# RWKV-6 attention and an MLP on one core: the first level of the decay tree of rounds 3 to 7 moves from the natural layout on GpSimd and VectorE back to TensorE

## The chip, the cores and the metric

The kernel runs on one core of a Trainium2 chip. The metric is device time in microseconds (us) of one launch, from inputs in the chip's memory to the output there; lower is better.

## The reference

Two blocks, one after the other, all in float32. The first is a linear attention with a state that decays per channel; its output, with the heads side by side, is the input of a layer norm, a ReLU MLP and a residual sum.

```python
# r, k, v, w: (4, 8, 768, 48); u: (8, 48); state: (4, 8, 48, 48), zero at first
for t in range(S):
    kt, vt, rt, wt = (k[:, :, t], v[:, :, t], r[:, :, t], w[:, :, t])
    cur = einsum('bhd,bhe->bhde', u[None] * kt, vt)
    y[:, :, t] = einsum('bhd,bhde->bhe', rt, state + cur)
    state = wt[:, :, :, None] * state + einsum('bhd,bhe->bhde', kt, vt)
x = y.transpose(0, 2, 1, 3).reshape(4, 768, 384)
mu, var = mean and variance of x over its last axis
xn = (x - mu) / sqrt(var + 1e-6) * g_ln
out = x + maximum(xn @ w_ch1, 0) @ w_ch2        # w_ch1: 384 x 1536, w_ch2: 1536 x 384
```

## The kernel before

**Units, rounds, levels.** A unit is four heads of one batch over half a sequence (384 steps); a round is the two units that make up all eight heads of those 384 steps, so there are 8 rounds (0 to 7) of units 2·round and 2·round + 1. Inside a unit the sequence is cut into chunks of 64 steps. What step s of a chunk gets from an earlier step t of the same chunk is the product r(s)·k(t), damped by the decays between them, and the kernel builds these 64 x 64 matrices (`A`) in six levels, like a tree. At level `lev` with n = 2^lev, neighbouring blocks of n steps are joined: `quads` (line 477) multiplies the keys with the queries of every second block on TensorE, 24 products for a unit (two matmul instructions each) into the PSUM tile `a_ps`; `grow` (497) multiplies the block's decays into `rkT` in place on VectorE; `keep` (514) takes from `a_ps` the entries that belong to this level and puts them into `A`. `totals` (391) multiplies the decays of pairs of blocks, level by level, on GpSimd.

**Around the levels.** `states` (578) forms the products k·v of each chunk (PSUM tile `kv`) and carries the state from chunk to chunk on VectorE (tile `s`); `outputs` (634) multiplies `A` with v and r with the states (PSUM tile `y`). Two PSUM buffers (pool `ps_a`) are taken in turn by `a_ps`, `kv` and `y`. The term with u of the same step is made in the natural layout, with the steps on the partitions: `own_products` (409) makes r·u·k on GpSimd, `own_sums` (423) reduces it on VectorE, `own_term` (460) multiplies the sums with v on GpSimd. From unit 2 on the inputs are loaded twice: natural (`load`, 122) and as runs that VectorE transposes (`stage`, 150; `squares`, 359).

**Level 0 in the natural layout.** From round 3 on (`FIRST = 3`, line 798), level 0 is not done by `quads`. Level 0 joins a step with the step before it, with no decay in between, and so it is an own term with k and v of the step before. `load_before` (170) loads k, and later v, shifted by one step, into the two buffers `nat["w"]`; `own_products` multiplies the shifted k with r; `own_sums` reduces it into `next` and zeroes the even steps with `odd`; `own_term` multiplies `next` with the shifted v and adds the result to `vo`. `keep` of level 0 then only zeroes the odd columns of `A`, once for each of its two buffers (rounds 3 and 4).

**The order.** Nearly everything is issued through wrappers that keep program order on its engine (`InOrder`, 39); only the loads and stores on SyncE's queue are ordered by the scheduler of the framework. The order is written out by hand: for each round (line 899) and each level (903), together a slot, numbered (round - 1)·6 + level, come the states or outputs of the round before, the quads of this level, `grow`, `keep`, and then a list of tasks for later rounds, which `fill` (766) spreads between steps of the MLP of the round before. An MLP step is six matmuls or so; a slot of the later rounds holds four. The MLP's first half is written to PSUM tile `h_ps`, the second to `o_ps`.

The places that the change touches in this order are the condition ahead of `quads` (916), the two loads of level 3 (977 to 979) and the two of the last level (994, 996).

Of the kernel before, what the change touches and what calls it, by code (L numbers as in the profile page):

```python
# [9 lines left out]
F32 = mybir.dt.float32  # L10
# [5 lines left out]
ALU = mybir.AluOpType  # L16
AX = mybir.AxisListType
# [35 lines left out]
def kernel(  # L53
# [13 lines left out]
    PE, ACT, DVE, POOL, SPO = (  # L67
        InOrder(tc, e) for e in (nc.tensor, nc.scalar, nc.vector, nc.gpsimd, nc.sync)
    )
    SP = nc.sync  # L70

    B, H, S, D = r.shape
    P = 128
    HP = 64
    C = 64
    NH = 4
    NP = NH // 2
    U = H // NH
    TT = 3
    RN = TT * P  # L80
# [13 lines left out]
    const = ctx.enter_context(tc.tile_pool(name="const", bufs=1))  # L94
    p1 = ctx.enter_context(tc.tile_pool(name="p1", bufs=1))
    p2 = ctx.enter_context(tc.tile_pool(name="p2", bufs=2))
# [10 lines left out]
    units = [(b, f, g) for b, f in rounds for g in range(U)]  # L107
# [3 lines left out]
    nat = {  # L111
        nm: [const.tile([P, TT, NH, HP], F32, name=f"nat_{nm}{i}") for i in range(2)]
        for nm in "wkr"
    }
# [35 lines left out]
    def stage(q, nm, pr, eng=SP):  # L150
# [4 lines left out]
        for j in range(2):  # L155
            first = src.offset + ((b * H + g * NH + 2 * pr + j) * S + f * RN) * D
            for e in range(HP // SQ):
# [8 lines left out]
                        tensor=src.tensor, offset=first + SQ * e, ap=[[NS * D, SQ], [1, n]]  # L166
                    ),
                )

    def load_before(q, src, i, eng=SP):  # L170

        b, f, g = units[q]
        for c in range(TT):
            eng.dma_start(
                out=nat["w"][i][:, c, :, 0:D],
                in_=bass.AP(
                    tensor=src.tensor,
                    offset=src.offset + ((b * H + g * NH) * S + f * RN + c * P - 1) * D,
                    ap=[[D, P], [S * D, NH], [1, D]],
                ),  # L180
            )

    def load_v(q, eng=SP):
        vn[q] = p4.tile([P, TT, NH, D], F32, tag="v", name=f"v{q}")
# [21 lines left out]
    for j in range(2):  # L206
        ACT.dma_start(
            out=sel[ds(HP * j, D), :, j], in_=u.rearrange("(r j) d -> j d r", j=2)[j]
# [4 lines left out]
    ident = const.tile([P, P], F32, name="ident")  # L213
# [11 lines left out]

    a_bufs = [const.tile([P, 2, U, NK, C], F32, name=f"A{i}") for i in range(2)]
    for t in a_bufs:
# [4 lines left out]
    for lev in range(NLEV - 1):  # L232
# [3 lines left out]
        for base, sign in ((0, 1), (n - 1, -1)):  # L236
            POOL.affine_select(
                out=m, in_=m, compare_op=ALU.is_ge, fill=0.0, base=base,
# [10 lines left out]
        out=bits0, in0=masks[0].rearrange("p q n -> p (q n)"), scalar1=-1.0, scalar2=None,  # L249
        op0=ALU.mult,  # L250
# [94 lines left out]
    st, carry = {}, {}  # L345
# [63 lines left out]
    def own_products(q, eng):  # L409
        b, f, g = units[q]  # L410
        rk = st[q]["ruk"] = p1.tile([P, TT, NH, D], F32, tag="rk", name=f"rk{q}")
        eng.tensor_tensor(
            out=rk, in0=nat["k"][q % 2][..., 0:D], in1=nat["r"][q % 2][..., 0:D], op=ALU.mult
        )
        eng.tensor_tensor(
            out=rk, in0=rk,
            in1=u_bc[:, ts(g, NH)][:, None].broadcast_to([P, TT, NH, D]), op=ALU.mult,
        )
        if q >= FIRST * U:
            k1 = nat["w"][0][..., 0:D]  # L420
            eng.tensor_tensor(out=k1, in0=k1, in1=nat["r"][q % 2][..., 0:D], op=ALU.mult)

    def own_sums(q):
        o = st[q]["own"] = p4.tile([P, TT, NH], F32, tag="own", name=f"own{q}")
        DVE.tensor_reduce(out=o, in_=st[q]["ruk"], axis=AX.X, op=ALU.add)
        if q >= FIRST * U:

            o = st[q]["next"] = p2.tile([P, TT, NH], F32, tag="next", name=f"next{q}")
            DVE.tensor_reduce(out=o, in_=nat["w"][0][..., 0:D], axis=AX.X, op=ALU.add)
            DVE.tensor_scalar(out=o, in0=o, scalar1=odd, scalar2=None, op0=ALU.mult)  # L430

    def products(q, eng=DVE):
        a = st[q]
# [26 lines left out]
    def own_term(q, eng):  # L460
        a = st[q]
        a["vo"] = p4.tile([P, TT, NH, D], F32, tag="vo", name=f"vo{q}")
        eng.tensor_tensor(
            out=a["vo"], in0=vn[q],
            in1=a["own"][:, :, :, None].broadcast_to([P, TT, NH, D]), op=ALU.mult,
        )
        if q >= FIRST * U:
            v1 = nat["w"][1][..., 0:D]
            eng.tensor_tensor(
                out=v1, in0=v1,  # L470
                in1=a["next"][:, :, :, None].broadcast_to([P, TT, NH, D]), op=ALU.mult,
            )
            eng.tensor_tensor(out=a["vo"], in0=a["vo"], in1=v1, op=ALU.add)

    a_ps = {}

# [36 lines left out]

    def keep(rnd, lev):
        n = 1 << lev
        A = a_bufs[rnd % 2]
        if lev == 0 and rnd >= FIRST:

            if rnd < FIRST + 2:
                DVE.memset(  # L520
                    A.rearrange("s j u k (q two) -> s (j u k) q two", two=2)[..., 1], 0.0
                )
            return
        ps = a_ps[rnd]
        if lev == NLEV - 1:
            for j in range(2):
                for i in range(2):
                    rows = ds(C * i, n)
                    late.append((A[rows, j, :, :, n:], ps[rows, j]))
        elif lev == 0:  # L530

            DVE.tensor_tensor(
                out=A.bitcast(I32).rearrange("s j u k (q two) -> s j (u k) q two", two=2)[..., 1],
                in0=ps.bitcast(I32).rearrange("s j u k q -> s j (u k) q"),
                in1=bits0[:, None, None].broadcast_to([P, 2, U * NK, C // 2]),
                op=ALU.bitwise_and,
            )
        else:
            DVE.copy_predicated(
                out=A.rearrange("s j u k (q two n) -> s j (u k) q two n", two=2, n=n)[:, :, :, :, 1],  # L540
                mask=masks[lev][:, None, None].broadcast_to([P, 2, U * NK, C // (2 * n), n]),
                data=ps.rearrange("s j u k (q n) -> s j (u k) q n", n=n),
            )
        if lev == NLEV - 1:
            for q in units_of(rnd):

                a = st[q]
                a["rx"] = p2.tile([P, NK, C], F32, tag="rx", name=f"rx{q}")
                R = a["r"].rearrange("p (k i t) -> p k i t", i=2, t=C)
                for j in range(2):  # L550
                    late.append((a["rx"][ds(HP * (1 - j), HP)], R[ds(HP * j, HP), :, 1, :]))
# [232 lines left out]
    def each(f, *ranges):  # L784
        calls = [()]
        for r_ in ranges:
            calls = [c + (x,) for c in calls for x in r_]
        return [lambda c=c: f(*c) for c in calls]
# [5 lines left out]
    def units_of(rnd):  # L794
        return [U * rnd + g for g in range(U)] if rnd < NR else []


    FIRST = 3
    odd = const.tile([P, 1], F32, name="odd")

    def take(eng, q):

        own_products(q, eng)
# [95 lines left out]
    for rnd in range(1, NR + 1):  # L899
        old, now, new = units_of(rnd - 1), units_of(rnd), units_of(rnd + 1)  # L900
        if rnd == 1:
            old = []
        for lev in range(NLEV):
            slot = (rnd - 1) * NLEV + lev
# [8 lines left out]
                if lev >= U and now:  # L913
                    mlp_step()
            for q in now:
                if slot and (lev or rnd < FIRST):
                    quads(q, lev)
            for which in ("rk",) if lev < NLEV - 1 else "kr":
                for q in now:
# [5 lines left out]
            tasks = []  # L925
            if rnd == 1:
                if lev < 2:
                    tasks += each(load, new, "kr"[lev], [SPO])
                if lev == 2:
                    SPO.dma_start(  # L930
                        out=u_bc,
                        in_=bass.AP(
                            tensor=u.tensor, offset=u.offset, ap=[[0, P], [D, H], [1, D]]
# [6 lines left out]
                    own_term(now[lev - 4], POOL)  # L940
            if rnd == 2 and lev == 0:
                tasks += each(load_v, now)
                DVE.tensor_reduce(
                    out=odd, in_=ident.rearrange("p (q two) -> p q two", two=2)[:, :, 1],
                    axis=AX.X, op=ALU.add,
                )
            if rnd == 2 and lev == 2:
                for q in now:
                    take(DVE, q)
# [22 lines left out]
            if lev == 3 and rnd > 1:  # L972
                for q in now:
                    load_vx(q)
                for q in new:
                    load_v(q)
                if new:
                    load_before(new[0], k, 0)
                    load_before(new[0], v, 1)
                if rnd > 2:  # L980
                    moments(rnd - 1)
                    tasks = each(norm, [rnd - 1]) + tasks
# [4 lines left out]
            if lev == NLEV - 1:  # L987

                if now:
                    mlp_step()  # L990
                if rnd >= 2 and new:
                    own_sums(new[0])
                if rnd >= 2:
                    tasks += each(load_before, new[1:], [k], [0])
                    tasks += each(own_term, new[:1], [POOL])
                    tasks += each(load_before, new[1:], [v], [1])
                    tasks += each(own_products, new[1:], [POOL])
                    tasks += each(own_sums, new[1:]) + each(own_term, new[1:], [POOL])
                    if new:
                        tasks += each(totals, [rnd + 1], [POOL])  # L1000
                if now:
                    tasks = mixed(
                        tasks,
                        each(ends, now, pairs) + each(finish, [2, 2, 4])
                    )
                if rnd == 1:
                    tasks = [join] * JOINS[lev] + tasks + each(totals, [rnd + 1], [POOL])
# [43 lines left out]
```

## Time and profile before

| | |
|---|---|
| median of 5 runs | 565.99 us (564.19 to 566.18) |
| profiled execution | 566.0 us, its span 564.3 us |
| TensorE busy (PE) | 546.9 us, 97% |
| VectorE busy (DVE) | 332.7 us, 59% |
| ScalarE busy (ACT) | 168.8 us, 30% |
| GpSimd busy (POOL) | 135.6 us, 24% |
| mean granted TensorE clock | 0.991 of full speed |

The span runs from the first to the last instruction of one profiled execution; the profiled execution's own time is 1.7 us longer. Every instruction is issued by one helper line (49), so groups of instructions are told apart by tile names and shapes: `a_ps<-rkT` are the quads, `rkT<-rkT,wT` and `rkT<-rkT,tot` are `grow`, `nat_w` is the buffer of the shifted k and v. A group's row gives busy us, mean ns of one, and after the second bar the idle time of the engine ahead of these instructions with what ended it. PE is TensorE's matmuls, PEld its weight loads, SPq SyncE's queue of DMA issues. The chain of waits is followed back from the last instruction; its rows are start us, length us, engine and tile.

### The profile page before, as it was taken

Reading aid. Unit: us, or ns where it says so; the run is one execution under the profiler, and the core shown is the slowest. Engines: PE = TensorE matmul, PEld = TensorE weight load, DVE = VectorE, ACT = ScalarE, POOL = GpSimd, SP = SyncE. Lnnn points to the kernel's source line nnn. Section 1 sums busy time; section 2 is a strip of 40 time slices with the busy share of each in tenths; the row PEclk is TensorE's granted clock in tenths of the full one; section 3 lists DMA queues with packets and bytes.
Section 4 is the critical chain, followed back from the end, with each engine's and each line's share of the span. In section 5 each row is a group of like instructions: output and inputs, shape, how many; then the busy total and the mean of one; then the engine's idle time right before and its main releaser. Section 6 shows DMA issues by size and latency. Waiting matters only on the chain.

```text
span 564.3 us, 18202 instructions
## 1 busy us (share of the span) xinstructions
PE 546.9 (97%) x7898; PEld 358.6 (64%) x7898; DVE 332.7 (59%) x654; ACT 168.8 (30%) x363; POOL 135.6 (24%) x157
## 2 busy tenths in 40 slices
PE   8999998998889999999999999999999999999997
PEld 6776665675556666666666666666666666665554
DVE  4888998859777785757387655666572611130000
ACT  2576887502250015201421026201521025202200
POOL 6140010204194019401580029022640000000000
PEclk9899999999997999999999999999999999999999
DMA  9958887245566565646464646546200000000000
GB/s 230 183 141 163 190 217 187 61 89 105 126 154 141 126 127 121 135 110 140 96 138 100 139 107 137 118 112 124 58 1 2 31 15 1 2 29 15 0 15 28
DMA packets 141552, 56.64 MB, mean 100 GB/s; under 512 B 124448, under 2 KB 130720, under 8 KB 141472
## 3 DMA queue, kind: packets, MB, share of 16 engines
q1 hardware_dynamic: 139600, 54.88, 43.6%
q8 instruction: 62, 1.02, 0.8%
q10 hardware_dynamic: 1872, 0.59, 0.4%
q14 instruction: 18, 0.15, 0.1%
HBM read 48.66 MB, written 4.72 MB: 95 GB/s over the span
## 4 chain that ended last, share of the span: by engine, by line
PE 82%; DVE 8%; ACT 3%; DMA 2%; SPq 2%; issue 2%; POOL 0%; ACTq 0%; DVEq 0%; POOLq 0%
PE o_ps L49 33%; PE h_ps L49 27%; PE a_ps L49 9%; PE y L49 4%; DVE rkT L49 2%; DVE w_sb L49 2%; PE kv L49 2%; PE kn_ps L49 2%; SPq L163 1%; ACT rest L49 1%; DMA nat_r<-in_r_dram 1%; PE xT_ps L49 1%; PE own_ps L49 1%; PE k_ps L49 1%; PE r_ps L49 1%
## 5 line engine op out<-in xcount | busy, mean ns | idle before, releaser
L49 PE MATMUL o_ps<-w_sb,h 128*128 128x384 f32 x576 | 199.7, 496 | 1.0 <-ACT h L49 1.0
L49 PE MATMUL h_ps<-xT,w_sb 128*128 128x384 f32 x576 | 196.5, 491 | 2.8 <-DVE o L49 1.4
L49 PEld LDWEIGHTS h_ps<-xT,w_sb 128*128 128x128 f32 x576 | 105.8, 190 | 70.4 <-DVE o L49 2.0
L49 PEld LDWEIGHTS o_ps<-w_sb,h 128*128 128x128 f32 x576 | 106.6, 192 | 67.3 <-ACT h L49 2.3
L49 DVE TENSOR_TENSOR rkT<-rkT,tot 128x768 f32<-128x768 f32 (+1 forms) x96 | 77.8, 852 | 27.7 <-issue 17.6
L49 ACT ACTIVATE h<-h_ps 128x384 f32<-128x384 f32 x96 | 46.9, 488 | 142.6 <-PE h_ps L49 142.4
L49 PEld LDWEIGHTS a_ps<-rkT 48*64 48x64 f32 x4128 | 65.6, 136 | 23.6 <-issue 12.1
L49 PE MATMUL a_ps<-rkT 48*64 48x32 f32 x4128 | 70.6, 222 | 3.5 <-DVE rkT L49 3.4
L49 DVE TENSOR_TENSOR o<-o_ps,x 128x384 f32<-128x384 f32 x24 | 13.3, 555 | 96.4 <-PE o_ps L49 96.3
L49 POOL TENSOR_TENSOR vo<-v,own 128x576 f32<-128x576 f32 x16 | 19.3, 1207 | 102.0 <-DVE own L49 60.7
L49 ACT ACTIVATE rstd<-mv,eps 128x3 f32<-128x3 f32 x8 | 2.4, 296 | 133.4 <-DVE mv L49 133.4
L49 POOL TENSOR_TENSOR nat_w<-nat_w,nat_r 128x576 f32<-128x576 f32 x10 | 15.8, 1578 | 105.2 <-DMA nat_w<-in_v_dram 71.4
L49 DVE SCALAR_TENSOR_TENSOR s<-s,decay,kv 128x48 f32<-128x48 f32 x160 | 29.3, 258 | 18.9 <-PE kv L49 18.9
L49 DVE COPY_PREDICATED A<-mask,a_ps 128x768 f32<-128x768 int8 x32 | 38.4, 1199 | 0.0
L49 DVE TENSOR_TENSOR x<-y,vo 128x288 f32<-128x288 f32 x32 | 13.2, 453 | 34.3 <-PE y L49 34.3
L49 ACT ACTIVATE xT<-xT_ps,g_sb 128x384 f32<-128x384 f32 x24 | 13.6, 579 | 48.4 <-PE xT_ps L49 48.4
L49 DVE TENSOR_TENSOR rkT<-rkT,wT 128x768 f32<-128x768 f32 x16 | 24.9, 1592 | 0.9 <-PE a_ps L49 0.8
L49 DVE TENSOR_REDUCE own<-rk 128x12 f32<-128x576 f32 x12 | 9.0, 750 | 23.5 <-POOL rk L49 23.5
L49 DVE TENSOR_SCALAR w_sb<-w_sb 128x384 f32<-128x384 f32 (+1 forms) x48 | 19.6, 408 | 0.8
L49 PEld LDWEIGHTS y<-v,A 64*64 64x64 f32 x384 | 12.8, 135 | 7.6 <-issue 4.4
L49 POOL TENSOR_TENSOR tot<-wT 128x768 f32<-128x768 f32 x6 | 12.4, 2074 | 21.1 <-DVE rkT L49 21.1
L49 PEld LDWEIGHTS kv<-v,kn 64*64 64x64 f32 x768 | 12.7, 135 | 7.5 <-issue 6.4
(88 smaller groups left out, 546.0 us busy)
## 6 DMA issues: line engine op xcount, KB each, us to landing
raw<-in_moe_w_ch_dram SPq DMA_DIRECT2D x24, 384.0 KB, 3.6
w_runs<-in_w_dram SPq DMA_DIRECT2D x79, 70.0 KB, 2.1
k_runs<-in_k_dram SPq DMA_DIRECT2D x79, 70.0 KB, 2.0
r_runs<-in_r_dram SPq DMA_DIRECT2D x79, 70.0 KB, 2.0
v<-in_v_dram SPq DMA_DIRECT2D x48, 96.0 KB, 3.0
out_dram<-o SPq DMA_DIRECT2D x24, 192.0 KB, 2.5
nat_r<-in_r_dram SPq DMA_DIRECT2D x42, 96.0 KB, 3.3
nat_k<-in_k_dram SPq DMA_DIRECT2D x42, 96.0 KB, 3.3
```

What stands on the lines that cost most here:

```text
L49: return lambda *args, **kw: self.tc.keep_in_program_order(f(*args, **kw))
L163: eng.dma_start(out=t[ds(HP * j + SQ * e, SQ), 0:n], in_=bass.AP(tensor=src.tensor, offset=first + SQ * e, ap=[[NS * D, SQ], [1, n]]),)
```

## The change

`FIRST` and all that hangs on it are removed. `quads` of level 0 and `keep` of level 0 (`A` from `a_ps` and a bit mask) run in rounds 3 to 7 as they do in rounds 0 to 2. The shifted loads, the second product, the second sum, the scaling by `odd`, and the two further operations of the own term go, with the constant `odd` and its one reduction, and with the two memsets of `A`. The rest of the order stays as written.

```diff
-    def load_before(q, src, i, eng=SP):
-        b, f, g = units[q]
-        for c in range(TT):
-            eng.dma_start(out=nat["w"][i][:, c, :, 0:D], in_=bass.AP(...))
...
     def own_products(q, eng):
...
-        if q >= FIRST * U:
-            k1 = nat["w"][0][..., 0:D]
-            eng.tensor_tensor(out=k1, in0=k1, in1=nat["r"][q % 2][..., 0:D], op=ALU.mult)
     def own_sums(q):
...
-        if q >= FIRST * U:
-            o = st[q]["next"] = p2.tile([P, TT, NH], F32, tag="next", name=f"next{q}")
-            DVE.tensor_reduce(out=o, in_=nat["w"][0][..., 0:D], axis=AX.X, op=ALU.add)
-            DVE.tensor_scalar(out=o, in0=o, scalar1=odd, scalar2=None, op0=ALU.mult)
     def own_term(q, eng):
...
-        if q >= FIRST * U:
-            v1 = nat["w"][1][..., 0:D]
-            eng.tensor_tensor(
-                out=v1, in0=v1,
-                in1=a["next"][:, :, :, None].broadcast_to([P, TT, NH, D]), op=ALU.mult,
-            )
-            eng.tensor_tensor(out=a["vo"], in0=a["vo"], in1=v1, op=ALU.add)
     def keep(rnd, lev):
         n = 1 << lev
-        A = a_bufs[rnd % 2]
-        if lev == 0 and rnd >= FIRST:
-            if rnd < FIRST + 2:
-                DVE.memset(
-                    A.rearrange("s j u k (q two) -> s (j u k) q two", two=2)[..., 1], 0.0
-                )
-            return
-        ps = a_ps[rnd]
+        A, ps = a_bufs[rnd % 2], a_ps[rnd]
...
-    FIRST = 3
-    odd = const.tile([P, 1], F32, name="odd")
...
             for q in now:
-                if slot and (lev or rnd < FIRST):
+                if slot:
                     quads(q, lev)
...
             if rnd == 2 and lev == 0:
                 tasks += each(load_v, now)
-                DVE.tensor_reduce(
-                    out=odd, in_=ident.rearrange("p (q two) -> p q two", two=2)[:, :, 1],
-                    axis=AX.X, op=ALU.add,
-                )
...
                 for q in new:
                     load_v(q)
-                if new:
-                    load_before(new[0], k, 0)
-                    load_before(new[0], v, 1)
...
                 if rnd >= 2:
-                    tasks += each(load_before, new[1:], [k], [0])
                     tasks += each(own_term, new[:1], [POOL])
-                    tasks += each(load_before, new[1:], [v], [1])
                     tasks += each(own_products, new[1:], [POOL])
```

## Prediction

> **What bounds the kernel now.** I read the page's busy shares first, then its slices, then the groups by line and shape, and last the chain of waits and the windows around the only stretch where the slices dip in mid-run.
>
> ```profile
> PE 546.9 (97%) x7898; PEld 358.6 (64%) x7898; DVE 332.7 (59%) x654; ACT 168.8 (30%) x363; POOL 135.6 (24%) x157
> PE   8999998998889999999999999999999999999997
> PEclk9899999999997999999999999999999999999999
> ```
>
> PE is the bound: 547 of 564 us. The slices (14.1 us each) say where the other 17 us are: slices 9 to 11 (127 to 169 us) show 8, from slice 12 on all is 9. The second line is the granted clock; slice 12 (169 to 183 us) has 7.
>
> ```profile
> L49 PE MATMUL a_ps<-rkT 48*64 48x32 f32 x4128 | 70.6, 222 | 3.5 <-DVE rkT L49 3.4
> L49 POOL TENSOR_TENSOR nat_w<-nat_w,nat_r 128x576 f32<-128x576 f32 x10 | 15.8, 1578 | 105.2 <-DMA nat_w<-in_v_dram 71.4
> L49 POOL TENSOR_TENSOR vo<-vo,nat_w 128x576 f32<-128x576 f32 x10 | 14.1, 1406 | 0.8
> L49 DVE TENSOR_REDUCE next<-nat_w 128x12 f32<-128x576 f32 x10 | 7.5, 748 | 3.9 <-POOL nat_w L49 2.6 <-DMA w_runs<-in_w_dram 1.3
> L49 DVE TENSOR_TENSOR A<-a_ps,bits 128x768 int32<-128x768 int32 x3 | 2.9, 952 | 0.0
> ```
>
> These rows price the exchange (busy us in total, then mean ns of one). `a_ps` is what `quads` writes: 4128 matmuls are 86 calls of 48 (16 units by 6 levels, less the ten that rounds 3 to 7 skip), so 70.6/86 = 0.82 us a call. The `nat_w` and `next` rows go; the `bits` row, `keep` at level 0, comes five times more.
>
> The chain of waits over the whole span shows what a call costs in its place:
>
> ```profile
> 218.25 0.84 PE kv L49 x48
> 219.10 7.94 PE h_ps L49 x24
> 227.04 0.84 PE kv L49 x48
> 227.88 1.39 PE a_ps L49 x96
> 229.27 7.94 PE h_ps L49 x24
> 240.88 1.53 PE a_ps L49 x96
> ```
>
> This is round 4 (slots 18 and 19). PE never waits here; the chain is PE after PE. In slot 18 `states` (kv) goes straight to the MLP; in slot 19 the quads of level 1 stand between. They take 1.39 us for both units, and the MLP's 24 matmuls after them the same 7.94. After an MLP matmul the same 96 take 1.53.
>
> The chain asked for 140 to 184 us shows the dip:
>
> ```profile
> 157.65 0.84 DVE rkT L49
> ...
> 159.43 3.04 DMA nat_w<-in_k_dram
> ...
> 162.59 1.42 POOL nat_w L49
> ...
> 164.03 0.76 DVE next L49
> ...
> 165.13 1.99 DVE s L49 x12
> 167.12 3.70 DVE rkT L49 x2
> ...
> 170.86 1.51 PE a_ps L49 x48
> 172.37 8.07 PE o_ps L49 x18
> ```
>
> The load of the shifted k for unit 7 is issued last in SP's queue, behind 32 run loads; POOL multiplies it, DVE's in-order queue stands at `next`, and `s` (the states of round 2) and `grow` of round 3 stand behind it. The PE timeline there has two idle gaps before `a_ps`, 1.84 us (to 168.81) and 1.15 (to 170.86), both put down to DVE rkT. Windows over the same place, the eighth figure being the clock:
>
> ```profile
> 168.50:172.00 3.50, 2.04 (x92) 1.96 (x94) 3.39 (x7) 0.00 (x0) 3.34 (x3) 0.67 0.61 132
> 172.00:174.00 2.00, 2.00 (x19) 1.33 (x15) 2.00 (x10) 0.69 (x2) 0.91 (x4) 0.50 0.65 122
> ```
>
> The clock falls to half after these gaps. It is back to 1.00 in the window from 178 us.
>
> **The change part by part.** *Added on PE.* Level 0 returns in rounds 3 to 7: ten `quads`, 480 matmuls, right behind `states(old[0])` in slots 12, 18, 24, 30 and 36. From 172 to 459 us PE has no idle, so every added us counts. I take 1.39 a round, as the nearest row (slot 19) is the same sequence kv, a_ps, h_ps: 5 x 1.39 = 6.95. Bounds: 1.39, and 1.53 plus the 0.19 that six o_ps take more after a_ps than otherwise (2.13 against 1.94), 1.72 a round or 8.6 in all.
>
> *Removed from PE's waits in slot 12.* Both gaps, 1.84 + 1.15 = 2.99 us, hang on `next`, which goes with its load. Rebuilt: DVE ends the last `squares` of unit 7 at 160.93 (it starts at 160.06, 0.87 long, held by the r runs, which SP issues ahead of the removed load, so it stays). `own_sums(7)` follows with no wait, as POOL needs 1.15 for vo from 155.1 and 1.42 + 1.40 for the products: 159.1. Then 0.75, `s` 2.0, so 163.7; two `grow` of level 0 at the slow 1.9 us each beside POOL's totals (3.77 the pair at 285 us), 167.5; `keep` 0.95, 168.5.
>
> PE meanwhile: kv ends 159.78, quads of unit 6 take 0.70, and those of unit 7 wait for the squares: a new stall of 160.93 - 160.48 = 0.45, say 0.5 (bounds 0 and 1.5, if the r runs land a us later). Then 1.39's rest, MLP 6.28, kv 0.85: level 1's quads are due at 168.8. They need `grow` (167.5) and the PSUM buffer of level 0's, freed by `keep` (168.5). So 0.3 us to spare, and I charge nothing; if POOL slows `keep` as well it is up to 1.
>
> *The clock.* At half clock 48 quads took 1.51 against 0.77 (half of 1.53), and 18 o_ps 8.07 against 6.00: 0.74 + 2.07 = 2.81 us. The gaps that precede it hold 2.99 idle us within four. The new stall is 0.5. A stall of 1.14 + 0.30 at 152 us was followed by a clock of 1.00, so I take the gain in full; bounds 0 and 2.81.
>
> A rule speaks against this part: the Trainium skill, TensorE: Matmul & The Clock Gate, HAM oscillation, says PE should avoid idle gaps of over about 3.4 us. No gap here is that long and the clock halved all the same, so the trace decides; by the rule alone the 2.81 would not belong to the gaps, and the sum would be 570.4.
>
> *DVE in rounds 4 to 7.* Out go two `next` reduces (0.75) and scalings (0.44), 2.4 us a round, and two memsets of 0.7 and one small reduce once. In comes `keep` at 0.95 a round, and with it a wait: `grow` must wait for the quads that read its operand, and level 1's quads for `keep`. Queued behind on DVE are the next states. In round 5 kv ends at 281.6, quads at 283.0; DVE: `s` 2.1, 283.8; `grow` 3.8, 287.6; `keep`, 288.6. PE reaches level 1's quads at 283.0 + 7.94 + 0.84 = 291.8. The cover is the MLP's 7.94 us, with 3.2 to spare: cost nothing. Without it, each us late costs 5. The PSUM buffer that level 0 takes is freed by ACT's A copies, at 280.2 against 281.6; 1.4 to spare.
>
> *POOL and SP.* Three POOL operations a unit go: 10 x (1.58 + 1.15 + 1.41) = 41 us, all off the path but the one above. 60 loads of 96 KB go from SP's queue, at about half a us to issue. What they stood ahead of, w runs, natural k and r for the round after, comes earlier; no PE gap depends on it, gain nothing. What they stood behind (k and r runs of round 3, from 141.89) starts with DVE's squares of w, so it doesn't move; the gaps at 136 (1.38) and 152 to 154 us (1.44) stay.
>
> **Sum**, against the profiled execution's 566.0 (span 564.3 plus 1.7, and the median of the runs is 565.99): + 6.95 + 0.5 - 2.99 - 2.81 = + 1.65, so 567.6.
>
> **The rivals.**
> *Clock stays bad* (0.15). The half clock returns, at the new stall or elsewhere at this stage: 567.6 + 2.8 = 570.4. For it: gaps of 1.4 at 152 us stay and 0.5 is added near by. Against: that stage kept 1.00 with the 1.4.
>
> *PE waits for `keep` or `grow` at level 1* (0.10): DVE's chain runs past the MLP cover by some 0.6 us a round, 5 x 0.6 = 3, so 570.6. Against: 3.2 us to spare in round 5. For: DVE operations double beside POOL, as `grow` shows (0.95 at 53.6 us, 1.9 at 285).
>
> *Half of it comes back* (0.13). Level 0's quads find unit 7's squares ready and the gap at 152 shrinks, as the 16 DMA engines carry less: 567.6 - 0.5 - 1.4 = 565.7, no change that can be measured. Against: SP issues those runs before the removed loads.
>
> *Faster* (0.12): SP's queue is the true bound of the whole stretch from 133 to 172 us. If the loads removed ahead of it let the natural k and r, and the runs behind them, start sooner, the gaps of 1.38 and 1.44 go as well as the 0.5: 567.6 - 3.3 = 564.3. It decides from the point where the k runs issue before 140 us. Against: they wait for DVE's squares of w (the chain has DVE wT up to 143.9), and the natural loads for DVE's products at 131.
>
> **How the numbers follow.** The forecast has 0.50, at 567.6, its own range 566.6 to 569.3 (below, no stall at the squares, 567.1, less half a us of the runs' own spread, 564.19 to 566.18; above, quads at 1.72, 5 x 0.33 more). What a measurement of this kernel can tell from no change is about 0.2%, 1.1 us: from 564.9 to 567.1. Of the forecast's half some 0.12 falls below 567.1. Slower: 0.38 + 0.15 + 0.10 = 0.63; same: 0.12 + 0.13 = 0.25; faster: 0.12. The range reaches from just under the "half" case to just over the slower rivals: 565.2 to 570.8.
>
> **What would show it.** `a_ps` at 4608 matmuls and about 78 us; PE busy up by some 7 less the 2.8 of the clock. In slots 18, 24, 30 and 36 kv, a_ps x96 at 1.39, h_ps x24 at 7.94 with no gap. In slot 12 a PE gap of about 0.5 before the second unit's quads, none over 0.3 before level 1's, and a clock of 1.00 from 165 to 180 us. The y of unit 4 starts at about 176.3 instead of 180.44. k runs still issued from 141.9. Wrong if the clock halves again, if the r runs move, or if PE shows gaps ahead of level 1's quads in rounds 4 to 7.

## The result and the profile after

The changed kernel's median is 567.69 us over 53 runs (565.24 to 570.29), against 566.39 over 95 runs of before (563.05 to 569.02). The ratio is 1.0022, 95% interval 1.0013 to 1.0032: slower by some 1.25 us (0.0022 x 566.4), where + 1.65 was forecast. The runs of both kernels spread over more than the difference, so it shows in the ratio and not in a pair of runs. The profiled execution took 566.56 us (span 564.5), only 0.56 more than that of before: its start was luckier, as its `kv` of unit 4, the last thing ahead of the first changed quads, begins at 158.15 us and not 158.93. In the profiles of the quads alone and of the clock without the wait (below), which change nothing ahead of it, it begins at 157.74 and 159.05, so 0.78 lies within what the start varies by.

The page after, the same lines (busy shares, then PE and the granted clock in 40 slices):

```profile
PE 550.5 (98%) x8378; PEld 363.9 (64%) x8378; DVE 315.6 (56%) x636; ACT 168.8 (30%) x363; POOL 92.7 (16%) x127
PE   8999998998899999999999999999999999999997
PEclk9899999999999999999999999999999999999999
```

PE is busy 3.6 us longer for 480 matmuls more, POOL 43 us less, DVE 17 less. The time freed on POOL and DVE buys nothing. The clock's 7 in slice 12 is gone, and so is PE's 8 in slice 11 (slices counted from 0). The window over the same place, the eighth figure being the clock:

```profile
165.00:180.00 15.00, 15.00 (x344) 10.10 (x345) 11.65 (x25) 2.70 (x6) 4.84 (x7) 1.00 0.71 145
```

The groups that price the exchange:

```profile
L49 PE MATMUL a_ps<-rkT 48*64 48x32 f32 x4608 | 77.7, 220 | 1.0 <-DVE rkT L49 0.7
L49 DVE TENSOR_TENSOR A<-a_ps,bits 128x768 int32<-128x768 int32 x8 | 7.6, 950 | 0.0
```

The quads' busy time rose from 70.6 to 77.7 us; "about 78" was forecast. The idle ahead of them fell from 3.5 to 1.0. The `next` rows and the `nat_w` products are gone, and `keep` of level 0 runs eight times and not three.

The chain of waits after, round 3 and then round 4 (start us, length us, engine and tile):

```profile
160.41 0.55 PE a_ps L49 x24
160.96 6.00 PE h_ps L49 x18
166.97 0.84 PE kv L49 x48
167.81 1.39 PE a_ps L49 x96
169.20 6.00 PE o_ps L49 x18
175.20 1.54 PE y L49 x88
...
213.01 0.84 PE kv L49 x48
213.85 1.39 PE a_ps L49 x96
215.24 7.94 PE h_ps L49 x24
```

From 160.41 us on PE runs for 300 us without a gap: the 18 `o_ps` take 6.00 and not 8.07 us, and the `y` of unit 4 begins 5.24 us earlier than in before (0.8 of that is the earlier start). Round 4 has the new quads in slot 18 at 1.39 us, as forecast, with the MLP's 7.94 unchanged after them. Four times 1.39 is 5.56, so the lead of 5.24 is spent by the end.

### The profile page after: what moved, and what is told of

Its sections match the earlier page's. It is cut to its first block, busy times and chain, and to the rows that moved or that the text cites. A ratio compares the mean times of both kernels' runs of the same rounds, so it can differ in the third digit from the quotient of the medians.

```text
span 564.5 us, 19007 instructions
## 1 busy us (share of the span) xinstructions
PE 550.5 (98%) x8378; PEld 363.9 (64%) x8378; DVE 315.6 (56%) x636; ACT 168.8 (30%) x363; POOL 92.7 (16%) x127
## 4 chain that ended last, share of the span: by engine, by line
PE 84%; DVE 7%; ACT 3%; DMA 2%; issue 2%; SPq 1%; ACTq 0%; DVEq 0%
PE o_ps L49 33%; PE h_ps L49 28%; PE a_ps L49 10%; PE y L49 4%; PE kv L49 2%; DVE w_sb L49 2%; PE kn_ps L49 2%; DVE rkT L49 2%; DMA nat_r<-in_r_dram 1%; ACT rest L49 1%; PE xT_ps L49 1%; SPq L163 1%; PE own_ps L49 1%; DMA r_runs<-in_r_dram 1%; PE k_ps L49 1%
## 5 line engine op out<-in xcount | busy, mean ns | idle before, releaser
L49 PE MATMUL o_ps<-w_sb,h 128*128 128x384 f32 x576 | 197.7, 492 | 1.1 <-ACT h L49 1.0
L49 PEld LDWEIGHTS a_ps<-rkT 48*64 48x64 f32 x4608 | 72.3, 135 | 21.1 <-issue 10.7
L49 PE MATMUL a_ps<-rkT 48*64 48x32 f32 x4608 | 77.7, 220 | 1.0 <-DVE rkT L49 0.7
L49 DVE STREAM_TRANSPOSE rkT<-r_runs 128x384 f32<-128x384 f32 x20 | 15.8, 846 | 6.2 <-DMA r_runs<-in_r_dram 6.2
L49 DVE TENSOR_TENSOR rkT<-rkT,wT 128x768 f32<-128x768 f32 x16 | 17.2, 1110 | 0.9 <-PE a_ps L49 0.8
L49 POOL TENSOR_TENSOR rk<-nat_k,nat_r 128x576 f32<-128x576 f32 x10 | 15.4, 1541 | 7.7 <-DMA nat_r<-in_r_dram 7.6
```

Source lines behind the costliest of these rows:

```text
L49: return lambda *args, **kw: self.tc.keep_in_program_order(f(*args, **kw))
```

## The experiments

Two things were to be told apart in a small net difference: what level 0 costs on TensorE, and what its natural form costs in round 3, as a wait and as a clock. Each ratio is to runs of before on the same chip, with its 95% interval.

**The quads alone.** Before, with the quads of level 0 issued in rounds 4 to 7 as well.

```diff
-                if slot and (lev or rnd < FIRST):
+                if slot and (lev or rnd != FIRST):
```

> Before, with the quads of level 0 issued as well in rounds 4 to 7 (their results are not used; round 3, keep and all else as in before). Theory: PE has no idle there, so each round pays 1.39 us: + 5.56, ratio 1.0098. In the trace kv, a_ps x96 of 1.39 and h_ps x24 of 7.94 with no gap. Rival (PE's 9s hide slack, or weight loads overlap): under + 2, ratio under 1.0035. Rival (the quads make `grow` late, so that level 1 waits): over + 8, ratio over 1.014.

Ratio 1.0097 (1.0069 to 1.0125), which is 5.5 us. The chain in round 4 has kv 0.84, a_ps 1.39, h_ps 7.94 with nothing between. Both rivals fall: PE's dense slices hide nothing, and `grow` isn't late.

**One round later.** Level 0 on TensorE in round 3, natural from round 4 on.

```diff
-    FIRST = 3
+    FIRST = 4
...
-                if new:
+                if new and rnd + 1 >= FIRST:
                     load_before(new[0], k, 0)
...
```

> Level 0 on TensorE in round 3 alone, in the natural layout from round 4 on. Theory: the wait on `next` in slot 12 is what the natural layout costs, and each later round it saves 1.39 us of PE. So against before: + 1.39 for the quads of round 3, + 0.3 for the squares they wait for, - 2.99 for the two gaps, - 2.8 where the clock is halved after them in before: - 4.1, ratio 0.9928; without the clock's part - 1.3, ratio 0.9977. Against the changed kernel it must be four times 1.39, 5.56, shorter. Rival (the natural layout saves nothing in the dense rounds): the time of the changed kernel, ratio 1.002.

562.84 us, ratio 0.9932 (0.9907 to 0.9957): - 3.9 us. Against the changed kernel it is 0.9932 - 1.0022, 0.9% or 5.1 us, where 5.56 was expected. So the natural layout pays in the four dense rounds, and in before its first round gave 3.9 of these 5.1 us back.

**The clock without the wait.** Before, with idle matmuls of zeros in the two gaps.

```diff
             for q in now:
                 if slot and (lev or rnd < FIRST):
+                    if rnd == 3 and lev == 1:
+                        warm(6 if q == now[0] else 3, "t")
                     quads(q, lev)
```

> Before, with idle matmuls of zeros put ahead of the quads of level 1 in round 3, where PE stands: 6 blocks of 128 columns ahead of unit 6 (about 1.3 us) and 3 ahead of unit 7 (0.65). They lie in the gaps of 1.84 and 1.15, so the wait on `next` stays. Theory (the clock halves because PE stands): the clock keeps 1.00 from 165 to 185 us, up to 2.8 us less: ratio 0.995 to 0.997, as not every run of before need be halved there. Rival (the clock falls wherever its window lies, or by the work of other engines): the half clock stays after 169 us, ratio 1.000.

563.37 us, ratio 0.9967 (0.9944 to 0.9991): - 1.9 us from work that computes nothing. PE's timeline shows that the wait is still there, only filled:

```profile
167.02 1.56 PE L49 MATMUL idle<-nought 128*128 128x384 f32 x4
168.58 0.90 PE L49 MATMUL a_ps<-rkT 48*64 48x32 f32 x48
169.41 0.91 PE L49 MATMUL idle<-nought 128*128 128x384 f32 x2
170.62 0.90 PE L49 MATMUL a_ps<-rkT 48*64 48x32 f32 x48 [0.30 <-DVE rkT L49]
171.46 6.07 PE L49 MATMUL o_ps<-w_sb,h 128*128 128x384 f32 x18
```

The second quads start at 170.62, in before at 170.86, so the wait on `next` is as long as it was. But they take 0.90 and not 1.51, and the `o_ps` 6.07 and not 8.14 (the same view of before). The twelve timed runs bear it out: by their mean clocks they spent 5.7 us at half clock on average, the runs of before on the same chip 11.8. With the waits of DVE, POOL and the loads as they were, the half clock here follows PE's standing still.

**The wait put back, first try.** The changed kernel, with the shifted k of unit 7 loaded, multiplied and summed ahead of the unit's own sums, unused.

```diff
+                    if rnd == 2:
+                        tasks += [lambda: hold_load(7)]
                     tasks += each(own_products, new[1:], [POOL])
+                    if rnd == 2:
+                        tasks += [lambda: hold(7)]
                     tasks += each(own_sums, new[1:]) + each(own_term, new[1:], [POOL])
```

> The changed kernel with the wait alone put back, in round 3 only: the shifted k of unit 7 is loaded, multiplied on POOL and reduced on DVE ahead of the unit's own sums, as in before; the result is not used, and level 0 stays on TensorE. Theory: DVE stands for this load again, so states, grow and keep of level 0 end some 4 us later, level 1's quads stand 2 to 3.5 us (they wait for keep's PSUM buffer too), and the clock is halved behind the gap in most runs: + 2.5 to + 6 against the changed kernel, ratio to before 1.007 to 1.013. Rival (in the changed kernel the order has slack enough, and the gap in before came from elsewhere): ratio 1.002 to 1.004, no gap over 0.5 ahead of level 1's quads.

Ratio 1.0029 (1.0008 to 1.0049): the expectation failed. The same load, product and sum cost nothing that can be measured (the changed kernel has 1.0022). The trace says why: with no other user of the buffer at that time the scheduler put the load's issues at 57.4 to 59.6 us, a hundred us early, and `next` ran on DVE at 162.58 without a wait for the load or for POOL. So it isn't the work that holds DVE; it is the lateness of the load.

**The wait put back, with its cause.** The same for units 6 and 7 through the one buffer that they share, as in before.

```diff
                 for q in new:
                     load_v(q)
+                if rnd == 2:
+                    hold_load(6)
...
                     own_sums(new[0])
+                    if rnd == 2:
+                        hold_sum(6)
...
+                        tasks += [lambda: hold_load(7)]
                     tasks += each(own_products, new[1:], [POOL])
+                        tasks += [lambda: hold_product(7), lambda: hold_sum(7)]
```

> The changed kernel with loads, POOL products and DVE sums of the shifted k of units 6 and 7 both put back in round 2, through the one buffer that before has for them, so that the load for unit 7 can't be issued until unit 6's sum has read the buffer; the results are not used, level 0 stays on TensorE. Theory (it is the shared buffer that makes the load late): the load lands at about 162 us, DVE stands for it, keep of level 0 ends 3 to 4 us later, level 1's quads stand 2 to 3.5 us and the clock is halved behind that in most runs: + 2.5 to + 6 against the changed kernel, ratio to before 1.007 to 1.013. Rival (the changed kernel's order absorbs it): ratio 1.002 to 1.004, no gap over 0.5.

572.89 us, ratio 1.0124 (1.0091 to 1.0158), the changed kernel plus about 5.8. The chain has the whole of it:

```profile
160.85 3.06 DMA nat_w<-in_k_dram
...
164.07 1.42 POOL nat_w L49
165.51 0.75 DVE next L49
...
166.93 1.99 DVE s L49 x12
168.91 2.98 DVE rkT L49 x2
171.90 0.87 DVE A L49
172.76 0.13 DVE s L49
172.91 2.79 PE a_ps L49 x96
175.70 7.65 PE o_ps L49 x18
```

PE stands 2.98 us ahead of level 1's quads. The profile puts this down to DVE s, queued right behind `keep` (DVE A); `grow` (DVE rkT) was over at 171.9, 1.0 us earlier. That it is `keep`'s release of level 0's PSUM buffer which counts is argued from the order and not shown. PE then pays the half clock: 2.79 for 1.39, 7.65 for 6.00. That is 2.98 + 1.40 + 1.65 = 6.0, against 5.8 measured. With the run before it this settles the chain: a buffer shared with unit 6 and so a late load, then POOL, DVE's in-order queue, PE, clock.

The buffer makes the load late by its place in SP's queue, and not by being held to the end. In before, unit 6's sum has read it by 155.73 us; SP issues the load at 157.98, as soon as it is through with the run loads (one row of DVE's timeline, two of SP's):

```profile
154.99 0.74 DVE L49 TENSOR_REDUCE next<-nat_w 128x12 f32<-128x576 f32 x1
154.00 3.88 SPq L163 DMA_DIRECT2D r_runs<-in_r_dram  x8
157.98 1.95 SPq L174 DMA_DIRECT2D nat_w<-in_k_dram  x3
```

In the run with the wait put back it is the same: read by 156.77, issued at 159.76, right behind the run loads. Why the scheduler chose this place isn't shown.

**The wait taken away, natural layout kept.** Before, with sums and own term of the second unit moved from the end of a round's last slot into the next round's level 0, behind `states`, `grow` and `keep`.

```diff
-                    tasks += each(own_sums, new[1:]) + each(own_term, new[1:], [POOL])
...
+            if rnd > 2 and lev == 0:
+                tasks += each(own_sums, now[1:]) + each(own_term, now[1:], [POOL])
```

> Before, with the sums and the own term of a round's second unit moved from the end of the slot ahead into the tasks of level 0, behind states, grow and keep. Level 0 stays in the natural layout from round 3 on; only DVE no longer stands at `next` ahead of the states. Theory: both gaps of slot 13 go (at most 0.3 left) and with them the half clock: - 2.7 to - 5.8, ratio 0.990 to 0.995, and against the changed kernel 1.25 more. Rival (the gaps come from the loads or from POOL, whatever DVE's order): level 1 still waits over 1 us, for totals or for squares, ratio above 0.998.

563.47 us, ratio 0.9967 (0.9942 to 0.9991): short of the 0.990 to 0.995 expected. Both gaps of slot 13, round 3's level 1, are gone (kv is followed by the quads at once), but PE's timeline has a new one, at 196 us where the old ones were at 167 to 171:

```profile
197.33 1.44 PE L49 MATMUL xT_ps<-ident,xn 128*128 128x128 f32 x6 [1.17 <-DVE xn L49]
198.60 3.79 PE L49 MATMUL o_ps<-w_sb,h 128*128 128x384 f32 x6
```

PE waits 1.17 us for the norm (`xn`), and the six `o_ps` after it take 3.79 us for 2.1: the half clock again. DVE was late because it stood at the r runs of unit 8 (1.21 and 1.60 us at 187 to 190 us), and these were issued behind 12 natural loads on SP.

**And the loads out of the way.** As the last, with the natural loads of k and r moved from level 1 to behind the stages of level 2.

```diff
-            if rnd > 2 and lev == 1:
-                tasks += each(load, new, ["kr"])
...
                 if m < 2:
                     tasks += each(stage, *turns[m + 1], pairs)
+            if rnd > 2 and lev == 2:
+                tasks += each(load, new, ["kr"])
```

> The run with the late sums, and in rounds from 3 on the natural loads of k and r for the round after moved from level 1 to behind the stages of level 2, so that the k and r runs of unit 8 no longer stand behind 12 load issues (7 us of SP). Theory: in the run with the late sums PE's gap of 1.17 us before xT (197 us) and the half clock behind it came from DVE waiting for these runs; they go. - 1.2 to - 3 against that run, ratio to before 0.990 to 0.994. Rival (the natural loads, now late, hold POOL's products and DVE's sums in slot 17 in their stead): a new DVE wait ahead of own, ratio 0.996 or above.

559.87 us, ratio 0.9893 (0.9867 to 0.9919): - 6.1 us against before, faster than both kernels, and a little better than the 0.990 to 0.994 expected: 4.2 us below the run before, where 1.2 to 3 were forecast. The gap ahead of `xT_ps` is gone, and the profile keeps full clock from 31 to 557 us. In the profile the gap had cost 1.17 us and 1.69 at half clock; what the runs gained beyond that is within the two intervals. The rival's wait does appear (DVE stands 5.04 us ahead of `next` in slot 17 at 209.85 us), but no PE gap comes from it: kv of slot 18 follows the MLP without one.

**The same loads in the changed kernel.**

> The changed kernel with the natural loads of k and r moved behind the stages of level 2, as in the run with the late loads. Theory: the changed kernel has no PE gap that comes from these loads, so its time stays: ratio to before 1.000 to 1.004; and it lies 5 x 1.39 + 0.3, 7.3 us, above the run with late sums and late loads (1.3%), which is the price of level 0 on TensorE with no wait on the other side. Rival (the moved loads, not the place of the sums, gave that run its gain): it falls with it, ratio 0.994 or below.

The edit is the last diff, on the changed kernel. 567.37 us, ratio 1.0017 (0.9993 to 1.0042): nothing, as expected. It lies 1.0017/0.9893, 1.25% or 7.1 us above the run before, give or take 2 by the two intervals; 7.3 were expected. So with that wait on neither side the change costs about its quads.

## Why the prediction was right

*Quads, + 6.95.* Right. 1.39 in each of the rounds 4 to 7 in the trace, 5.5 for four in the run with the quads alone. The bound with switches, 1.72, did not come up.

*The squares, + 0.5.* 0.31: DVE ends the last r run of unit 7 at 160.37, and PE, through with 72 of the 96 quads at 160.10, stands for it. The stall was forecast from unit 6's quads alone, but half of unit 7's need not wait. SP issues the k runs first at 140.97 (141.89 in before, in an execution 0.9 later there), so the condition of the rival "faster", an issue before 140, is not met; the gaps at 135.7 us (1.36) and 152.3 us (1.28) stayed.

*The gaps, - 2.99* (they stand at level 1, in slot 13, and not in slot 12). Right, none ahead of level 1's quads. `grow` was overpriced, 3.07 for the pair and not 3.8: POOL's widest total (128x768) ran beside it for only 0.76 us, where in before it did for the whole 2.19. So `keep` had 0.9 us to spare rather than 0.3.

*The clock, - 2.81.* Right in the profile, where the 96 quads and 18 `o_ps` are at full clock again. One reading was off: the clock fell before the second gap was over, and not after both. In before it reads 1.00 from 168.80 to 169.60 us, behind the gap of 1.84, and 0.50 from 169.80 to 170.80, while PE stands in the gap of 1.15. For the average over executions there is an estimate. Each timed run carries its mean clock; (1 - clock) x span x 2 is the time at half clock. Over 63 runs of before, taken with the experiments, it is 12.4 us (clock 0.982 to 0.994), over 54 of the changed kernel 6.2 (0.988 to 1.000). A line through half time and span of the runs gives 559.8 + 0.38 per us for before, 563.8 + 0.29 for after. At full clock (which no run of before reached) that is + 4.0 for the change, where the terms without the clock sum to + 4.46; the clock's part is 1.8 - 4.7, some - 2.8. With one slope for both kernels it is + 3.2 and some - 2.1, so the split is known to within a us or so. The rival "the clock stays bad" fails on average; other half-clock stretches remain, in the start above all.

*Round 3 as a whole.* From the `kv` of unit 4 to its `y` the changed kernel takes 4.46 us less (5.24 less the 0.78 of the start), where the terms of this round give 3.91 (1.39 + 0.5 - 2.99 - 2.81). Against the 5.56 of rounds 4 to 7 that leaves + 1.1, and the runs have + 1.25.

*The cover in rounds 4 to 7, nothing.* Right: 1.39 and 7.94 are all that PE shows, so `keep` and `grow` are never waited for. The cover was wider than reckoned: in rounds 4, 6 and 7 POOL, without the operations of the natural level 0, was past its big totals before `grow` began, and the pair took 1.8 to 1.9 us and not 3.8; in round 5 it took 3.06.

What the prediction did not say is why the load was late. It saw it "issued last in SP's queue", which is where the trace has it. The two runs with the wait put back show what sets this place: with the buffer shared by both units the load is issued at 160 us, without at 57.

## What to carry to other kernels

Where one engine is dense, work taken from it was worth its row here, and work given to it cost that row; idle engines paid for neither. What ate the gain was the first round, where the new producer is not yet ahead: look there for an in-order queue that stands at the new operation with the critical work behind it, and move that operation behind it before giving the idea up. Price a short gap on TensorE with the half-speed stretch that may follow it.

## What the runs showed of the hardware

The gaps of 1.84 and 1.15 us in before, one of 2.98 in the run with the wait put back and one of 1.17 in the run with the late sums each went with half clock, some 3.4 to 6.8 us long, costing another 1.5 to 3 us. The length of a gap does not decide it alone. At 152 to 157 us every profile of this case has a gap of 1.11 to 1.57 us and one of 0.30: half clock followed in one of the ten, with 1.57 (level 0 natural a round later), where the six `h_ps` there took 3.66 us and not 2.1. It did not follow 1.50, nor the 1.36 to 1.38 at 135 to 140 us in any profile. What does decide it isn't shown. The time at half clock varies between runs of the same program (7 to 20 us in before, by the mean clocks); with zeros fed to TensorE in the gaps the profile kept full clock there. The Trainium skill, TensorE: Matmul & The Clock Gate, HAM oscillation, warns of gaps of over about 3.4 us; these were all shorter, so here its limit is too wide.

DVE's `grow` of level 0 takes 0.95 us alone (1.82 the pair at 52.8 us) and 1.6 to 2.2 beside POOL's operations in round 3 of before (3.77 the pair), so an operation's duration depends on what POOL does then. It can also be POOL that pays: in before a product of 128x576, 1.41 us otherwise, took 2.90 at 387.6 us, while DVE's pair beside it kept to 1.80.
